# A Fourier mixing layer and a routed expert layer on one core: GpSimd's time in the planner's due times, the tile ramp made once, a larger reserve of expert work

## The chip, the cores and the metric

The kernel runs on one core of a Trainium2 chip. The metric is device time in microseconds (us). The time before is the median of three runs. Everything is float32. Engine names are those of the profile: PE (TensorE matmuls), PEld (its weight loads), DVE (VectorE), ACT (ScalarE), POOL (GpSimd), SP (SyncE, which here issues the ordinary DMAs).

## The reference, cut to what matters

```python
# x (8, 2496, 256), filt_r and filt_i (1249, 256)
X = np.fft.rfft(x, axis=1)
Y = X * (filt_r + 1j * filt_i)[None]
x = np.fft.irfft(Y, n=2496, axis=1).astype(np.float32).reshape(19968, 256)
# w_gate (256, 8), w1 (8, 256, 1024), w2 (8, 1024, 256)
logits = x @ w_gate
expert_idx = np.argmax(logits, axis=1)
probs = softmax(logits)                      # with 1e-9 added to the sum
gate_w = probs[np.arange(N), expert_idx]
for e in range(8):                           # on the tokens of expert e
    y[tokens] = np.maximum(x[tokens] @ w1[e], 0.0) @ w2[e]
return gate_w[:, None] * y                   # (19968, 256)
```

## The kernel before, in words

**Fourier part.** A sequence of 2496 is cut as 39 by 64, and the transform is done with four kinds of matmul steps for each of the 8 batches. `stage_a` (line 324) does the 39-point transforms, `stage_b` (line 337) the 64-point ones with the twiddle factors, followed on DVE by the product with the filter; `stage_c` (line 361, and 359 for the first pair) goes back over 64 points and `stage_d` (line 382) over 39. Between A and B the data makes a round trip through DRAM (`zd`), between C and D another (`ud`), and D's result is stored to `yd`. `turn_y` (line 395) transposes it and `logits` (line 408) multiplies it by the gate weights. The loads land in tiles called `fin` (8 buffers); what A, C and D leave for their stores (`zo`, `uo`, `yo`) shares 6 buffers, so the copy out of PSUM for a seventh such tile waits for the first one's stores.

**Routing.** When a batch is done, `route` turns its logits into a row of a table in DRAM for each token. It has a chain of small DVE operations, two matmuls `rk` (lines 444 and 445) in the midst of it, and at its end 22 indirect DMAs on GpSimd (line 485), each of which scatters 8 bytes for each of up to 117 tokens (30 DMAs in the last batch). Then `tile_map` works out, in one-row DVE operations, which expert and which table row each tile of 512, 256 or 128 tokens has. There are 65 tiles: 1, 6, 2, 5, 5, 5, 5 and 36 for the eight batches, which are called batch 0 to batch 7 here.

**Experts.** For a tile, SP reads its list of tokens from the table (`listed`, line 574, into `idt`). Its DMA waits for all the scatters that stand before it in the program. GpSimd gathers the tokens' rows from `yd` (`gather`, line 590, one indirect DMA for 128 rows, into `xg`, 2 buffers), PE transposes them (`turn_x`, line 617), multiplies by the expert's `w1` (`hidden`, line 624) and by `w2` (`result`, line 639), and GpSimd scatters the gated rows to the output (line 644). The weights, 1 MB each for a tile, are loaded by SP (lines 609 and 605).

**What sets the order.** The program is a planner that writes out PE, DVE, ACT and SP by hand, in the order in which it runs; on GpSimd a scheduler keeps nearly the same order. The loop at the end takes one step after the other, either of the Fourier part or of the experts, and advances a clock `now` by the step's price (for instance 0.43 us for a `hidden` of 128 columns, 3.42 for a `result`). An expert step may be taken when the thing it needs is due: `prefetch` notes in `when`, at each issue, `now` plus a constant of `GAP` (5 us for a list, 7 for a gather, 9 for weights). `share` says how much expert work goes between Fourier steps, from what is known and not done, less `RESERVE`. After each step, `side` is called twice and advances `route` or `tile_map` to its next `yield`.

Of the kernel before, what the change touches and what calls it, by code (L numbers as in the profile page):

```python
# [10 lines left out]
F32 = mybir.dt.float32  # L11
I32 = mybir.dt.int32
U32 = mybir.dt.uint32
AF = mybir.ActivationFunctionType
ALU = mybir.AluOpType
# [7 lines left out]
E = 8  # L23
# [110 lines left out]
def kernel(  # L134
# [15 lines left out]
    nc = tc.nc  # L150
# [9 lines left out]
    for b in range(B):  # L160
        GROUPS.append([])
        for rows, most in WANT[b]:
            n = min(most, max(0, ((b + 1) * S - (N - left) - E * (rows - 1)) // rows))
# [14 lines left out]
    perm = ctx.enter_context(tc.tile_pool(name="perm", bufs=1))  # L178
# [3 lines left out]
    eoff = perm.tile([P, E], F32, name="eoff")  # L182
    done = perm.tile([1, E], F32, name="done")
    one = perm.tile([1, E], F32, name="one")
    moe = ctx.enter_context(tc.tile_pool(name="moe", bufs=2))
    ps = ctx.enter_context(tc.tile_pool(name="ps", bufs=7, space=PSUM))

    fft = ctx.enter_context(ExitStack())
    cst = fft.enter_context(tc.tile_pool(name="cst", bufs=1))
# [15 lines left out]
    ids0 = cst.tile([TP, NG], F32, name="ids0")  # L205
    vld = cst.tile([TP, NG], F32, name="vld")
    e_i = cst.tile([P, E], I32, name="e_i")

    def bank():
        return ps.tile([P, 512], F32, tag="bank", name="bank")  # L210


    now = [0.0]
    free = {"v": 0.0, "s": 0.0}

    def either(n, on_vector, on_scalar):

        v = max(free["v"], now[0]) + 0.1 + n / 960
        s = max(free["s"], now[0]) + 0.2 + n / 1200
        if v <= s:  # L220
            free["v"] = v
            on_vector()
        else:
            free["s"] = s
            on_scalar()

    def evac(o, i, n):
        either(n, lambda: nc.vector.tensor_copy(o, i), lambda: nc.scalar.copy(out=o, in_=i))  # L228

    HP = P // 2  # L230
    CH = [(i0, min(4, NG - i0)) for i0 in range(0, NG, 4)]
# [22 lines left out]
    def make_constants():  # L254
        make_identity(nc, ident)
        nc.gpsimd.memset(ones, 1.0)
        nc.gpsimd.affine_select(
            out=tri, in_=ones[:, :TP], compare_op=ALU.is_gt, fill=0.0, base=0, pattern=[[1, TP]], channel_multiplier=-1
        )
        nc.gpsimd.memset(seg, 1.0)  # L260
        nc.gpsimd.memset(seg[:, :, 0:1], 0.0)
        nc.gpsimd.memset(cnt, 0.0)
        nc.gpsimd.memset(fill[:, 0:1], N)
        nc.gpsimd.memset(fill[:, 1:2], 0)
        nc.gpsimd.iota(prow, pattern=[[0, 1]], base=0, channel_multiplier=1)
        nc.gpsimd.iota(e_i, pattern=[[1, E]], base=0, channel_multiplier=0)
        nc.vector.tensor_scalar(em8, in0=e_i, scalar1=-float(E), scalar2=None, op0=ALU.add)
        nc.vector.tensor_scalar(eoff, in0=e_i, scalar1=float(TE), scalar2=None, op0=ALU.mult)
        nc.vector.memset(done, 0.0)
        nc.vector.memset(one, 1.0)  # L270
# [17 lines left out]
    def mark(key):  # L288
        moves[1].append(lambda: stored.add(key))
# [118 lines left out]
                    mm(lgs[b][:TP, 0, t * E:(t + 1) * E], lhsT=yt[:, 2 * i + dh, :], rhs=wg[:, dh, :],  # L408
                       start=(dh == 0), stop=(dh == DH - 1))

    scatters = {}


    def route(b):
# [3 lines left out]
        she = (TP, E, NG)  # L418
# [55 lines left out]
        rows = [(row[:N1 if t == NG - 1 else TP, t:t + 1], pay[:N1 if t == NG - 1 else TP, t, :]) for t in range(NG)]  # L474
        if b == B - 1:
# [5 lines left out]
            nc.vector.tensor_copy(pad, padf)  # L481
            rows += [(pad[:, e:e + 1], fill) for e in range(E)]
        scatters[b] = []
        for t, (at, what) in enumerate(rows):
            sc = nc.gpsimd.indirect_dma_start(  # L485
                out=table,
                out_offset=bass.IndirectOffsetOnAxis(ap=at, axis=0),
                in_=what,
                in_offset=None,
            )  # L490

            tc.declare_no_dep(sc.ins, group="scatter", reason="rows of their own")
            tc.declare_no_dep(sc.ins, group="listed", reason="rows of their own")
            tc.add_to_no_dep_group("scatter", sc.ins)
            scatters[b].append(sc.ins.name)
            if t % 2:
                yield


    def tile_map(b, rows, n, last):  # L500
# [3 lines left out]
        end = moe.tile([1, E], F32, name="end", bufs=1)  # L504
# [14 lines left out]
        nc.vector.tensor_tensor(add, add, base, op=ALU.subtract)  # L519
        nc.vector.tensor_tensor(add[:, :E - 1], add[:, :E - 1], base[:, 1:], op=ALU.add)  # L520
        yield
        tau_i = moe.tile([1, n], I32, tag=f"tau_i{n}", name="tau_i", bufs=1)
        tau = moe.tile([1, n], F32, tag=f"tau{n}", name="tau", bufs=1)
        nc.gpsimd.iota(tau_i, pattern=[[1, n]], base=0, channel_multiplier=0)
        nc.vector.tensor_copy(tau, tau_i)
        past = moe.tile([1, n, E - 1], F32, tag=f"past{n}", name="past", bufs=1)
        she = (1, n, E - 1)
        nc.vector.tensor_tensor(
            past, tau[:, :, None].to_broadcast(she), end[:, None, :E - 1].to_broadcast(she), op=ALU.is_ge
        )  # L530
        yield
        ef = moe.tile([1, n], F32, tag=f"ef{n}", name="ef", bufs=1)
# [5 lines left out]
        rf = moe.tile([1, n], F32, tag=f"rf{n}", name="rf", bufs=1)  # L538
        rrow = moe.tile([1, n], I32, tag=f"rrow{n}", name="rrow", bufs=2)
        nc.vector.tensor_reduce(rf, past, axis=AX.X, op=ALU.add)  # L540
        nc.vector.tensor_scalar(tau, in0=tau, scalar1=float(rows), scalar2=base[:, 0:1], op0=ALU.mult, op1=ALU.add)
        nc.vector.tensor_tensor(rf, rf, tau, op=ALU.add)
        if last:

# [86 lines left out]
    def result(i, j):  # L631
        n, e, r, b = work[i]
        ids = idt[i]
        if i >= SHORT:
            ev = nc.tensor.value_load(e, min_val=0, max_val=E - 1)
        p = bank()
        for k in range(FT):
            w2 = late["w2s"][:, bass.ds(ev, 1), k, :] if i >= SHORT else w2t[i][:, k, :]
            mm(p[:, :D], lhsT=hs[i][k][:, j * P:(j + 1) * P], rhs=w2, start=(k == 0), stop=(k == FT - 1))  # L639
        ys = moe.tile([P, D], F32, tag="ys", name="ys", bufs=4)  # L640
        gate = ids.bitcast(F32)[:, j, 1:2]
        either(D, lambda: nc.vector.tensor_scalar(ys, in0=p[:, :D], scalar1=gate, scalar2=None, op0=ALU.mult),  # L642
               lambda: nc.scalar.activation(ys, p[:, :D], AF.Copy, scale=gate))
        nc.gpsimd.indirect_dma_start(  # L644
            out=out,
            out_offset=bass.IndirectOffsetOnAxis(ap=ids.bitcast(U32)[:, j, 0:1], axis=0),
            in_=ys,
            in_offset=None,
            bounds_check=N - 1,
            oob_is_err=False,  # L650
        )
# [74 lines left out]
    got = {"list": 0, "x": 0, "w1": 0, "w2": 0}  # L726
    used = {"x": 0, "w1": 0, "w2": 0}
    when = {}
    GAP = {"list": 5.0, "x": 7.0, "w1": 9.0, "w2": 9.0}

    def prefetch():

        def may(what, depth):
            i = got[what]
            deep = depth if i < SHORT else 4
            return i < len(work) and i - used.get(what, used["w1"]) < deep
        def mark(what):
            when[what, got[what]] = now[0] + GAP[what]
            got[what] += 1
        if may("list", 3):  # L740
            listed(got["list"])
            mark("list")
        i = got["x"]
        if i < got["list"] and i - used["x"] < 2 and when["list", i] <= now[0]:
            gather(i)
            mark("x")
        for what in ("w1", "w2"):
            if got[what] < got["list"] and may(what, 2):
                weights(got[what], what == "w2")
                mark(what)  # L750
# [23 lines left out]
        return min(4.0, max(0.3, (known - RESERVE) / max(left_t[0], 1.0)))  # L774


    RESERVE = 40.0
    with tc.manual_schedule(
        engines={mybir.EngineType.PE, mybir.EngineType.DVE, mybir.EngineType.Activation, mybir.EngineType.SP}
    ):  # L780
# [62 lines left out]
```

## Time and profile before

| | |
|---|---|
| median of 3 runs | 1778.86 us (1777.88 to 1785.63) |
| profiled execution: its own time | 1779.41 us |
| profiled execution: span of the instructions | 1777.7 us |
| mean granted TensorE clock | 0.954 |
| PE busy | 1618.0 us, 91% of the span, 7126 records |
| DVE, ACT, POOL busy | 554.2, 318.0, 504.3 us |
| DMA | 296.16 MB, mean 167 GB/s |

In the records of PE a float32 matmul of the program stands as two, a transposition as one. Busy time of PE is not yet work done, since a matmul takes about twice as long while the granted clock is 0.5. So the profile is read in two steps: where PE stands idle and for whom, and at which clock it worked afterwards.

### The profile page before, as it was taken

Reading aid. Unit: us, or ns where it says so; the run is one execution under the profiler, and the core shown is the slowest. Engines: PE = TensorE matmul, PEld = TensorE weight load, DVE = VectorE, ACT = ScalarE, POOL = GpSimd, SP = SyncE. Lnnn points to the kernel's source line nnn. Section 1 sums busy time; section 2 is a strip of 40 time slices with the busy share of each in tenths; the row PEclk is TensorE's granted clock in tenths of the full one; section 3 lists DMA queues with packets and bytes.
Section 4 is the critical chain, followed back from the end, with each engine's and each line's share of the span. In section 5 each row is a group of like instructions: output and inputs, shape, how many; then the busy total and the mean of one; then the engine's idle time right before and its main releaser. Section 6 shows DMA issues by size and latency. Waiting matters only on the chain.

```text
span 1777.7 us, 21069 instructions
## 1 busy us (share of the span) xinstructions
PE 1618.0 (91%) x7126; PEld 1183.5 (67%) x7126; DVE 554.2 (31%) x1328; ACT 318.0 (18%) x575; POOL 504.3 (28%) x536
## 2 busy tenths in 40 slices
PE   3897695999997899979999799999999999999997
PEld 1464463877665566656676567676767668889997
DVE  0755362255351112512125122313101002334443
ACT  1332121122221122212222121212121210000000
POOL 0003123215225220342115312445523222222221
PEclk7898897999998899989999899999999999999999
DMA  8888778568758452754425523542434335554551
GB/s 298 259 258 206 220 185 236 199 188 205 240 120 195 149 184 75 183 175 135 123 91 129 177 97 110 147 139 81 131 140 174 145 132 186 193 197 168 176 178 42
DMA packets 120965, 296.16 MB, mean 167 GB/s; under 512 B 32338, under 2 KB 73028, under 8 KB 105893
## 3 DMA queue, kind: packets, MB, share of 16 engines
q1 hardware_dynamic: 99322, 252.77, 47.0%
q0 software_dynamic: 21536, 42.03, 7.4%
q8 instruction: 58, 0.95, 0.2%
q14 instruction: 49, 0.40, 0.1%
HBM read 212.74 MB, written 82.88 MB: 166 GB/s over the span
## 4 chain that ended last, share of the span: by engine, by line
PE 76%; DMA 11%; issue 4%; POOL 4%; DVE 3%; SPq 1%; ACT 0%; POOLq 0%; DVEq 0%; ACTq 0%
PE bank L639 30%; PE bank L624 29%; PE lg L408 3%; POOL table L485 3%; PE bank L337 3%; DMA fin<-ud 3%; PE bank L382 2%; PE bank L361 2%; PE bank L324 2%; DMA xg<-yd,idt 2%; PE bank L617 2%; DMA zd<-zo 2%; PE bank L395 2%; DMA table<-pay,row 1%; DMA ud<-uo 1%
## 5 line engine op out<-in xcount | busy, mean ns | idle before, releaser
L624 PE MATMUL bank<-xT,w1t 128*128 128x512 f32 (+2 forms) x2080 | 595.4, 438 | 0.1
L639 PE MATMUL bank<-w2t,hT 128*128 128x256 f32 x2240 | 502.2, 382 | 0.0
L624 PEld LDWEIGHTS bank<-xT,w1t 128*128 128x128 f32 x2080 | 340.1, 192 | 203.9 <-issue 183.8
L639 PEld LDWEIGHTS bank<-w2t,hT 128*128 128x128 f32 x2240 | 424.8, 191 | 61.9 <-issue 5.3
L644 POOL DMA_INDIRECT out_dram<-ys,idt x163 | 162.6, 998 | 683.4 <-DVE ys L642 352.0
L485 POOL DMA_INDIRECT table<-pay,row x176 | 173.5, 986 | 289.0 <-DVE row L471 184.7
L590 POOL DMA_INDIRECT xg<-yd,idt x163 | 157.6, 967 | 288.8 <-PE bank L617 201.7
L628 ACT ACTIVATE hT<-bank 128x512 f32<-128x512 f32 (+1 forms) x235 | 138.0, 587 | 490.2 <-PE bank L624 490.2
L642 DVE TENSOR_SCALAR ys<-bank,idt 128x256 f32<-128x256 f32 x150 | 72.5, 483 | 482.4 <-PE bank L639 454.6
L617 PE MATMUL bank<-ident,xg 128*128 128x128 f32 x326 | 53.8, 292 | 77.3 <-DMA xg<-yd,idt 77.1
L627 DVE TENSOR_SCALAR hT<-bank 128x128 f32<-128x128 f32 (+1 forms) x285 | 96.5, 339 | 80.7 <-PE bank L624 77.6
L337 PE MATMUL bank<-fin,tbs 128*128 128x256 f32 (+1 forms) x320 | 90.4, 405 | 26.0 <-issue 25.1
L228 DVE COPY xT<-bank 128x512 f32<-128x512 f32 (+2 forms) x64 | 30.9, 483 | 266.1 <-PE bank L617 266.1
L617 PEld LDWEIGHTS bank<-ident,xg 128*128 128x128 f32 x326 | 41.3, 148 | 96.5 <-issue 82.7
L382 PE MATMUL bank<-fin,tds 117*117 117x256 f32 (+1 forms) x352 | 89.2, 393 | 15.4 <-DMA fin<-ud 15.4
L337 PEld LDWEIGHTS bank<-fin,tbs 128*128 128x128 f32 (+1 forms) x320 | 61.1, 199 | 58.1 <-issue 47.7
L324 PE MATMUL bank<-fin,tas 117*117 117x512 f32 x176 | 91.6, 647 | 6.2 <-DMA fin<-in_x_dram 6.1
L382 PEld LDWEIGHTS bank<-fin,tds 117*117 117x117 f32 (+1 forms) x352 | 64.4, 187 | 46.5 <-issue 27.5
L228 ACT COPY xT<-bank 128x512 f32<-128x512 f32 (+2 forms) x66 | 28.1, 428 | 370.3 <-PE bank L617 266.3
L344 DVE TENSOR_TENSOR ys<-bank,ht 128x512 f32<-128x512 f32 x80 | 55.1, 688 | 123.1 <-PE bank L337 123.0
L408 PEld LDWEIGHTS lg<-wg,yt 128*117 128x117 f32 x704 | 79.5, 183 | 9.7 <-issue 5.6
L361 PE MATMUL bank<-ys,tcs 128*128 128x512 f32 x144 | 75.2, 604 | 10.3 <-DVE ys L347 6.9
(97 smaller groups left out, 893.0 us busy)
## 6 DMA issues: line engine op xcount, KB each, us to landing
w1t<-in_moe_w_dram SPq DMA_DIRECT2D x65, 1024.0 KB
w2t<-in_moe_w_dram SPq DMA_DIRECT2D x42, 1024.0 KB
fin<-in_x_dram SPq DMA_DIRECT2D x40, 512.0 KB
zd<-zo SPq DMA_DIRECT2D x120, 156.0 KB
fin<-ud SPq DMA_DIRECT2D x120, 156.0 KB
yd<-yo SPq DMA_DIRECT2D x120, 156.0 KB
fin<-zd SPq DMA_DIRECT2D x72, 256.0 KB
ud<-uo SPq DMA_DIRECT2D x72, 256.0 KB
```

What stands on the lines that cost most here:

```text
L324: mm(p[:TP, :], lhsT=tas, rhs=xt[:TP, j:j + 2, :], start=True, stop=True)
L337: mm(p[:, i * D:(i + 1) * D], lhsT=tbs[:k, f + i, :], rhs=zi[:k, j + i, :], start=True, stop=True)
L361: mm(p, lhsT=tcs[:, 1, :], rhs=ys, start=True, stop=True)
L382: mm(p[:TP, i * D:(i + 1) * D], lhsT=tds[:k, i0 + j + i, :], rhs=ui[:k, j + i, :], start=True, stop=True)
L408: mm(lgs[b][:TP, 0, t * E:(t + 1) * E], lhsT=yt[:, 2 * i + dh, :], rhs=wg[:, dh, :], start=(dh == 0), stop=(dh == DH - 1))
L485: sc = nc.gpsimd.indirect_dma_start(out=table, out_offset=bass.IndirectOffsetOnAxis(ap=at, axis=0), in_=what, in_offset=None,)
L590: nc.gpsimd.indirect_dma_start(out=xgs[i][:, j], out_offset=None, in_=yd[0:rows, :], in_offset=bass.IndirectOffsetOnAxis(ap=idt[i].bitcast ...
L617: nc.tensor.transpose(pt[:, j, :], xg[:, j, dh * P:(dh + 1) * P], ident)
L624: mm(p[:, :m], lhsT=w1t[i][:, dh, k * P:(k + 1) * P], rhs=xts[i][:, dh, :m], start=(dh == 0), stop=(dh == DH - 1))
L628: lambda: nc.scalar.activation(hT[:, :m], p[:, :m], AF.Relu))
L639: mm(p[:, :D], lhsT=hs[i][k][:, j * P:(j + 1) * P], rhs=w2, start=(k == 0), stop=(k == FT - 1))
L644: nc.gpsimd.indirect_dma_start(out=out, out_offset=bass.IndirectOffsetOnAxis(ap=ids.bitcast(U32)[:, j, 0:1], axis=0), in_=ys, in_offset=No ...
```

## The change

It has four parts. The constants of `GAP` for lists and gathers go, and the planner keeps a clock for GpSimd (`free["p"]`, advanced by `pool`, 1.3 us for each indirect DMA): a list is due 5 us after the scatters of its batch are, a gather 3.5 us after GpSimd's clock has passed it. `route` gives control back after 8 scatters instead of 2, so that the 22 scatters stand in the program in one or two places instead of six, and `tile_map` and the batch's first lists come earlier. The ramp 0, 1, 2, ... that `tile_map` needs is made once at the start (`tau0`), where each call had made its own on GpSimd and cast it on DVE. `RESERVE` goes from 40 to 60 us.

```diff
+    tau0 = perm.tile([1, 64], F32, name="tau0")
...
-    free = {"v": 0.0, "s": 0.0}
+    free = {"v": 0.0, "s": 0.0, "p": 0.0}
...
+    def pool(start, n):
+
+        free["p"] = max(free["p"], start) + 1.3 * n
+        return free["p"]
...
+        nc.gpsimd.iota(tau_i, pattern=[[1, 64]], base=0, channel_multiplier=0)
+        nc.vector.tensor_copy(tau0, tau_i)
...
         scatters[b] = []
+        rows_at[b] = pool(now[0] + 5.0, len(rows)) + 3.0
...
-            if t % 2:
+            if t % 8 == 7:
                 yield
...
-        tau_i = moe.tile([1, n], I32, tag=f"tau_i{n}", name="tau_i", bufs=1)
         tau = moe.tile([1, n], F32, tag=f"tau{n}", name="tau", bufs=1)
-        nc.gpsimd.iota(tau_i, pattern=[[1, n]], base=0, channel_multiplier=0)
-        nc.vector.tensor_copy(tau, tau_i)
...
         gate = ids.bitcast(F32)[:, j, 1:2]
+        pool(now[0], 1)
...
-    GAP = {"list": 5.0, "x": 7.0, "w1": 9.0, "w2": 9.0}
...
-        def mark(what):
-            when[what, got[what]] = now[0] + GAP[what]
+        def mark(what, at=None):
+            when[what, got[what]] = at or now[0] + 9.0
             got[what] += 1
         if may("list", 3):
-            listed(got["list"])
-            mark("list")
+            i = got["list"]
+            listed(i)
+            mark("list", max(now[0], rows_at[work[i][3]]) + 5.0)
...
             gather(i)
-            mark("x")
+            mark("x", pool(now[0], work[i][0]) + 3.5)
...
-    RESERVE = 40.0
+    RESERVE = 60.0
```

What this does to the order is shown at three places. The names are those of the profile; the line numbers of the changed kernel are 7 to 9 higher, so that its `turn_x` is L624, its `hidden` L631 and its `result` L646. A row stands for one kind of instruction, with its count behind the x.

The first place is PE in the routing of batch 4, up to the transposition of that batch's first tile (the last row). In the kernel before, these are the last twelve of the 21 rows that follow `rk`:

```order
L361 MATMUL bank<-ys,tcs 128x512
L382 MATMUL bank<-fin,tds 117x256 x4
L395 MATMUL bank<-ident,yo 128x117 x8
L324 MATMUL bank<-fin,tas 117x512 x2
L624 MATMUL bank<-xT,w1t 128x512 x6
L337 MATMUL bank<-fin,tbs 128x256 x2
L624 MATMUL bank<-xT,w1t 128x512 x4
L361 MATMUL bank<-ys,tcs 128x512
L624 MATMUL bank<-xT,w1t 128x512 x4
L382 MATMUL bank<-fin,tds 117x256 x4
L624 MATMUL bank<-xT,w1t 128x512 x2
L617 MATMUL bank<-ident,xg 128x128 x8
```

In the changed kernel, the last twelve of the 29 rows that follow `rk`, up to the same tile:

```order
L404 MATMUL bank<-ident,yo 128x117 x8
L646 MATMUL bank<-w2t,hT 128x256 x8
L333 MATMUL bank<-fin,tas 117x512 x2
L646 MATMUL bank<-w2t,hT 128x256 x8
L631 MATMUL bank<-xT,w1t 128x512 x4
L346 MATMUL bank<-fin,tbs 128x256 x2
L631 MATMUL bank<-xT,w1t 128x512 x2
L370 MATMUL bank<-ys,tcs 128x512
L631 MATMUL bank<-xT,w1t 128x512 x4
L391 MATMUL bank<-fin,tds 117x256 x4
L631 MATMUL bank<-xT,w1t 128x512 x6
L624 MATMUL bank<-ident,xg 128x128 x8
```

Before the batch's first transposition there now stand a whole `hidden` and a whole `result` of the tile ahead of it and a part of the next tile's `hidden`.

The second place is SP in the routing of batch 0, around the batch's first list (`idt`). Before:

```order
L316 DMA fin<-ud 39x4x256 x3
L286 DMA yd<-yo 39x1024 x3
L309 DMA fin<-zd 64x1024
L310 DMA fin<-zd 64x1024
L286 DMA zd<-zo 39x4x256 x3
L303 DMA fin<-in_x_dram 128x512
L316 DMA fin<-ud 39x4x256 x3
L286 DMA yd<-yo 39x1024 x3
L316 DMA fin<-ud 39x2x256
L316 DMA fin<-ud 39x256 x2
L572 TENSOR_LOAD rrow
L572 ISA x2
```

And in the changed kernel, from the same load of `ud` on:

```order
L325 DMA fin<-ud 39x4x256 x3
L295 DMA yd<-yo 39x1024 x3
L318 DMA fin<-zd 64x1024
L319 DMA fin<-zd 64x1024
L579 TENSOR_LOAD rrow
L579 ISA x2
L581 ISA
L581 DMA idt<-table 128x4
L609 TENSOR_LOAD erow
L609 ISA x2
L616 ISA
L616 DMA w1t<-in_moe_w_dram 128x2048
```

The list has moved ahead of a store of `zd`, a load of `x`, two loads of `ud` and a store of `yd`, which now follow it and the two weight loads.

The third place is SP in the routing of batch 1. Before, from a load of `x` on:

```order
L303 DMA fin<-in_x_dram 128x1024
L286 DMA zd<-zo 39x4x256 x3
L286 DMA ud<-uo 64x1024
L286 DMA ud<-uo 64x768
L316 DMA fin<-ud 39x4x256 x3
L286 DMA yd<-yo 39x1024 x3
L309 DMA fin<-zd 64x1024
L310 DMA fin<-zd 64x1024
L286 DMA zd<-zo 39x4x256 x3
L303 DMA fin<-in_x_dram 128x512
L316 DMA fin<-ud 39x4x256 x3
L286 DMA yd<-yo 39x1024 x3
```

And in the changed kernel, from the same load on:

```order
L312 DMA fin<-in_x_dram 128x1024
L579 TENSOR_LOAD rrow
L579 ISA x2
L581 ISA
L581 DMA idt<-table 128x8
L609 TENSOR_LOAD erow
L609 ISA x2
L616 ISA
L616 DMA w1t<-in_moe_w_dram 128x2048
L609 TENSOR_LOAD erow
L609 ISA x2
L612 ISA
```

Before, the list of batch 1 follows these twelve rows; now it stands right behind the load of `x`, and all the stores and loads of the other rows follow it.

## Rows read from the trace of the kernel before

**Rows 1.** Waits of PE: who waited for whom, us, times, longest.
```profile
PE bank L617 <- DMA xg<-yd,idt: 77.1, 17, 16.1
```
**Rows 2.** Timeline of PE, batches 1, 3, 4: start, length, what, records, idle before.
```profile
244.79 0.53 PE L444 MATMUL rk<-oe,tri 117*117 117x176 f32 x2 [2.12 <-DVE oe L435]
...
515.39 0.59 PE L444 MATMUL rk<-oe,tri 117*117 117x176 f32 x2 [2.12 <-DVE oe L435]
...
585.04 1.33 PE L617 MATMUL bank<-ident,xg 128*128 128x128 f32 x5 [0.64 <-DMA xg<-yd,idt]
...
732.17 0.53 PE L444 MATMUL rk<-oe,tri 117*117 117x176 f32 x2 [2.38 <-DVE oe L435]
...
739.73 3.62 PE L639 MATMUL bank<-w2t,hT 128*128 128x256 f32 x16
743.18 1.88 PE L324 MATMUL bank<-fin,tas 117*117 117x512 f32 x4
744.90 1.03 PE L337 MATMUL bank<-fin,tbs 128*128 128x256 f32 x4
745.77 1.02 PE L361 MATMUL bank<-ys,tcs 128*128 128x512 f32 x2
746.63 1.89 PE L382 MATMUL bank<-fin,tds 117*117 117x256 f32 x8
748.36 0.96 PE L395 MATMUL bank<-ident,yo 117*128 117x117 f32 x8
749.15 1.88 PE L324 MATMUL bank<-fin,tas 117*117 117x512 f32 x4
750.88 5.31 PE L624 MATMUL bank<-xT,w1t 128*128 128x512 f32 x12
756.03 1.03 PE L337 MATMUL bank<-fin,tbs 128*128 128x256 f32 x4
...
780.20 0.45 PE L617 MATMUL bank<-ident,xg 128*128 128x128 f32 x1 [11.98 <-DMA xg<-yd,idt]
```
**Rows 3.** Timeline of POOL, batch 4: first and last scatter, ramp, first gather.
```profile
739.18 0.98 POOL L485 DMA_INDIRECT table<-pay,row  x1 [10.58 <-DVE row L471]
...
767.51 0.89 POOL L485 DMA_INDIRECT table<-pay,row  x1 [0.30 <-issue]
768.42 0.13 POOL L524 IOTA tau_i<- 1x5 int32 x1
...
772.79 0.99 POOL L590 DMA_INDIRECT xg<-yd,idt  x1 [4.24 <-DMA idt<-table]
```
**Rows 4.** Five stretches: length, busy (records) PE PEld DVE ACT POOL, clock, DMA.
```profile
189.30:208.50 19.20, 3.87 (x12) 2.95 (x12) 1.54 (x3) 2.03 (x4) 1.96 (x2) 0.56 0.81 280
282.00:304.10 22.10, 4.44 (x11) 2.31 (x11) 1.38 (x2) 2.25 (x4) 6.20 (x8) 0.61 0.79 262
565.00:590.80 25.80, 7.21 (x15) 3.49 (x15) 0.69 (x1) 1.18 (x2) 12.87 (x14) 0.54 0.85 279
768.20:785.40 17.20, 4.15 (x13) 3.01 (x13) 0.69 (x1) 1.18 (x2) 4.18 (x6) 0.60 0.77 245
978.90:997.00 18.10, 6.47 (x19) 4.76 (x19) 0.69 (x1) 1.18 (x2) 3.84 (x4) 0.62 0.74 259
```
**Rows 5.** SP's line of the lists: semaphore waits, ns min/median/max; scatters' time to landing.
```profile
L574 SPq EVENT_SEMAPHORE  x122: 17/28/26921, 192.8 to 1728.4; - x122
...
DMA to landing us min/median/max: 2.5/7.7/12.5
```
**Rows 6.** Timelines of SP and POOL, batches 0 and 1: list's new neighbour, last scatter.
```profile
180.88 0.79 SPq L310 DMA_DIRECT2D fin<-zd  x1
...
182.21 0.90 POOL L485 DMA_INDIRECT table<-pay,row  x1 [0.30 <-issue]
...
257.14 0.36 SPq L303 DMA_DIRECT2D fin<-in_x_dram  x1
...
282.18 0.89 POOL L485 DMA_INDIRECT table<-pay,row  x1 [0.30 <-DMA zd<-zo]
```
**Rows 7.** A stretch of Fourier work alone, columns as in rows 4.
```profile
100.00:145.00 45.00, 41.47 (x220) 29.81 (x218) 27.01 (x46) 14.49 (x27) 0.00 (x0) 0.96 0.85 255
```

More of the change, by code (lines that the diff above doesn't have):

```diff
@@ L207 @@
     e_i = cst.tile([P, E], I32, name="e_i")
+    tau_i = cst.tile([1, 64], I32, name="tau_i")
     def bank():
@@ L409, in logits @@
                        start=(dh == 0), stop=(dh == DH - 1))
-    scatters = {}
+    scatters, rows_at = {}, {}
     def route(b):
@@ L528, in tile_map @@
         nc.vector.tensor_tensor(
-            past, tau[:, :, None].to_broadcast(she), end[:, None, :E - 1].to_broadcast(she), op=ALU.is_ge
+            past, tau0[:, :n, None].to_broadcast(she), end[:, None, :E - 1].to_broadcast(she), op=ALU.is_ge
         )
@@ L540, in tile_map @@
         nc.vector.tensor_reduce(rf, past, axis=AX.X, op=ALU.add)
-        nc.vector.tensor_scalar(tau, in0=tau, scalar1=float(rows), scalar2=base[:, 0:1], op0=ALU.mult, op1=ALU.add)
+        nc.vector.tensor_scalar(tau, in0=tau0[:, :n], scalar1=float(rows), scalar2=base[:, 0:1], op0=ALU.mult, op1=ALU.add)
         nc.vector.tensor_tensor(rf, rf, tau, op=ALU.add)
```

## The prediction

> **What bounds the kernel now.** PE is busy 91% of the span, so I looked first for whom it waits. One line of that list is large: the first transposition of a tile, which waits for its gathered rows, 77.1 us in 17 waits [rows 1]. The timeline of PE shows where. In batch 4, `rk` starts at 732.17, and at 780.20 the first transposition comes after 11.98 us of idling [rows 2]. The timeline of POOL says why: the first scatter starts 7 us after `rk`, the last at 767.51, and the gather can only start at 772.79, when the list has been read [rows 3]. From the first scatter to the last, 767.51 - 739.18 = 28.3 us go for 22 indirect DMAs (one output scatter among them), 1.29 us each, and that is most of the way. The same happens in batches 0, 1, 3 and 5, and after each stop the clock is at 0.5 for some us more. Rows 4 has the five stretches, each from PE's stop to the clock's return.
>
> What such a stretch loses is its length less the work done in it. The busy part lies at half clock, so the work is half of it: 19.2 - 1.9 = 17.3, 22.1 - 2.2 = 19.9, 25.8 - 3.6 = 22.2, 17.2 - 2.1 = 15.1 and 18.1 - 3.2 = 14.9 us [rows 4]. Together that is 89.4 us: 37.2 in batches 0 and 1, 52.2 in batches 3, 4 and 5.
>
> **How much work stands between.** The prices of PE's steps are differences of starts [rows 2]: `result` 3.45 for 16 records, A 1.72 for 4, B 0.87 for 4, C 0.86 for 2, D 1.73 for 8, `turn_y` 0.79 for 8, `hidden` 5.15 for 12. In matmuls of the program (two records each, a transposition one) that is 0.43 for B, D and `result`, 0.86 for A, C and a `hidden` of 512 columns, 0.10 for a `turn_y`; a transposition of 128 columns I take at 0.14. In batch 4 before, there stand between `rk` and the first transposition of the batch's first tile 16 `hidden` (13.8), 8 `result` (3.4), 6 A (5.2), 8 B (3.5), C for 3.4, 12 D (5.2), `turn_y` 0.8 and `rk` 0.6, in all 36 us. From 732.17 on that ends at 768.2, and that is where PE stops (780.20 - 11.98). So the prices hold, and what decides is this cover against the 48 us that the gathers took.
>
> In the changed order the same place has 32 `hidden` (27.5), 32 `result` (13.8), a tile's transpositions (1.1) and the same Fourier steps: 61 us. Counted in the same way, the cover before and after is 28 and 52 us in batch 0, 30 and 54 in 1, 61 and 93 in 2, 48 and 63 in 3, 36 and 61 in 4, 36 and 61 in 5, 59 and 68 in 6, 124 and 126 in 7.
>
> **The change part by part.** *Due times for lists and gathers.* In batch 4 the gathers' data came 48 us after `rk` began and the last piece some 2.5 us later; 61 covers that with 10 to spare. Batch 5 is alike. In batch 3 the last piece came at 585.04, 69.7 us after `rk` [rows 2], because output scatters stood between on POOL. 63 us do not cover that. But the list stands earlier now and the output scatters that still stand between belong to work that PE has done before, so I take zero there and 7 us as the bad end. So the 52.2 us of the three late batches go. In batches 0 and 1 the gathers' waits of 37.2 us go too, since 52 and 54 us of work at that place take longer than 52 us on the clock: PE took from 244.79 to 282.0, 37.2 us, for 29.7 us of such work [rows 2, 4].
>
> *Scatters in one place, lists earlier.* This is what the change adds. SP's instruction for the list waits until the scatters that stand before it have landed, and everything behind it on SP waits too. Such a wait lasted up to 26.9 us before [rows 5]. In batch 0 SP reaches the list's new place at 181.7 (the end of the `zd` load); the last scatter starts at 182.21 and lands 2.5 us (least) to 7.7 us (median) later, so SP stands for 3 to 8 us [rows 5, 6]. In batch 1 the new neighbour is the `x` load at 257.14, the last scatter starts at 282.18: SP stands for 27 to 32 us, until 40 to 45 us after `rk` [rows 5, 6]. Behind it wait stores of `zd` and `ud`, loads of `ud`, `zd` and `x`, and the weights.
>
> What PE can do meanwhile follows from the order. The first step that needs something behind the list comes 24 us of PE work after `rk` in batch 0 (a copy into the six shared buffers, whose `zd` store waits), 29 in batch 1 (the same, with a `ud` store), 54 in batch 2, 77 to 80 in batches 3 to 6, and 55 in batch 7, where only weights wait. A small DMA that was issued behind two weight loads took 780.20 - 772.79 = 7.4 us [rows 2, 3]. So the missing thing is there 47 to 52 us after `rk`: in time for batches 2 to 6, too late for 0 and 1. In batch 7 thirty scatters make it 8 x 1.29 = 10 us later, 57 to 62 against 55, for a weight load that is two tiles ahead in the order; I take zero and 6 as the bad end. Batch 0: PE reaches its place about 4 us before 189.3 [rows 4], at 185, and gets on at 192 to 197; 7 to 12 us, I take 8. Batch 1: it reaches 29 us of work about 36 us after `rk` and gets on at 47 to 52; 11 to 16, I take 13. After each, some 2 us at half clock, as in rows 4. In all 25 us given back. The values are near the short ends because SP and the transfers run late in these batches anyway.
>
> The Trainium skill ("DMA: Bandwidth & Descriptors", Anatomy of one DMA) says that DMA engines do not wait on semaphores and that any such wait happens on the issuing sequencer before dispatch. By that rule the wait stops the whole queue, and the 26.9 us of rows 5 agree; if the wait went along with its own DMA, the 25 us would fall away and the sum would be 1693.
>
> *A larger reserve.* PE's work is the same in amount and no path gets longer by it; it moves expert work from batches 0 to 2 to later. In batch 0, 52 instead of 28 us of nearly pure Fourier work follow `rk`. Such work runs at 41.47 / 45 = 0.92 busy and a clock of 0.96, so at 0.885 of full rate, beside a DMA share of 0.85 [rows 7]. 24 us more of it lose 24 / 0.885 - 24 = 3 us; the ends are 0 (if it fills holes that experts would fill) and 9 (three batches).
>
> *The ramp.* Eleven short instructions each on POOL and DVE become one. One took 0.13 us on POOL [rows 3], right behind the last scatter, where POOL then waits for the list; zero, and 10 x 0.13 = 1 us if that cover went. `tile_map`'s DVE operations come a few steps earlier in DVE's queue, the same in number, on an engine that is busy 31% of the span; zero.
>
> **Sum**, against the profiled execution's own 1779.4 us (0.6 above the median, so I make no difference): 1779.4 - 89.4 + 25 + 3 = 1718.
>
> **The rivals.** *A: the early gain is eaten up.* The transfers are the limit in batches 0 and 1 (share 0.79 to 0.85 in rows 4 and 7), so that what PE no longer waits for gathers it waits for `ud`, `zd` and stores. Then only the late 52.2 us go, less up to 7 in batch 3 and some 10 for a longer stop: 1727 to 1750, about 1737. For it speaks that SP's queue stands 30 us in a stage with little expert work; against it that PE was busy 0.92 of the time in a stretch of Fourier work alone, so that the transfers nearly keep up [rows 7].
>
> *B: nothing is given back.* SP's stops lie beside queued transfers, as those of 26.9 us did in the kernel before. 1779.4 - 89.4 = 1690, with 0 to 9 for the thinner mix up to 1699.
>
> *C: slower.* SP's stop reaches PE in every batch. The point from which it decides: the list is released later than PE can work, so beyond 77 us after `rk` instead of 40 to 45. Then six batches lose 26.9 + 2 us and batch 0 some 8: 1779.4 - 89.4 + 6 x 28.9 + 8 + 3 = 1874. Nothing in the order speaks for it, unless scatters land far later than 7.7 us.
>
> *D: the due times do not do what they say.* The gathers stay as late relative to PE as before, because POOL stands behind output scatters longer than 1.3 us each, as in batch 3. Half of the late 52.2 stays: 1744.
>
> *E: no difference*, because other work moves into the stops and is missed later: 1775 to 1785. Against it, PE's idle time has no other large owner [rows 1].
>
> **How the numbers follow.** The forecast (1700 to 1735) 0.53; A 0.21; B 0.12; C 0.05; D 0.05; E 0.04. The range takes in the forecast, A to its end and nearly all of B: 1692 to 1750. A measurement of this kernel tells about 0.5%, 9 us, from no change: faster 0.90, within 0.04, slower 0.06.
>
> **What would show it.** Right: in the profile after, PE's waits for `xg` under 15 us in all, none of more than 7 in batches 3 to 5, and the clock at full from some 400 us on; SP's waits at the list near 27 us in most batches; two new idle places of PE of 8 and 13 us in batches 0 and 1, for loads, or for DVE or ACT with a store before them. Wrong: stops of PE for `fin` or weights in batches 3 to 7 (C); `xg` still over 30 us (D); `rk` of batch 2 no earlier on the clock for the same amount of work done (A).

## The result, and the profile after

The changed kernel takes 1723.6 us (median of 4 runs, 1719.3 to 1731.9) against 1779.2 for the kernel before: ratio 0.969, 95% interval 0.964 to 0.973. The forecast was 1718. The profiled execution of the changed kernel is the longest of its four, 1731.9 us of its own time with a span of 1730.2, so it is to be read against 1779.4 of before: 47.5 us less.

PE's list of waits, the one that rows 1 are from (who waited for whom; us in all, times, longest), no longer has a line for `xg`. Of the longest that are left behind the start, the three lines that end in `ACT zo` or `ACT yo` are new; before, such a wait came to 0.2 us in all:

```profile
PE bank L404 <- ACT zo L230: 17.8, 2, 15.2
PE rk L453 <- DVE oe L444: 11.5, 5, 3.0
PE bank L391 <- DMA fin<-ud: 11.4, 4, 4.5
...
PE bank L370 <- ACT zo L230: 8.5, 1, 8.5
PE bank L391 <- ACT yo L230: 5.4, 2, 4.5
```

Line 230 is the copy out of PSUM, here into the six shared `st` buffers: PE stands because ACT stands, and ACT stands because a buffer's store has not gone out, as ACT's timeline shows for the second stop:

```profile
291.64 0.59 ACT L230 COPY zo<-bank 117x512 f32<-117x512 f32 x1 [21.19 <-DMA zd<-zo]
```

The timeline of PE (start, length, what, records, idle time before) has the three places, one in batch 0 and two in batch 1, and then batch 4, where [rows 2] had an idle time of 11.98 us ahead of the first transposition:

```profile
205.50 2.08 PE L370 MATMUL bank<-ys,tcs 128*128 128x512 f32 x2 [8.45 <-ACT zo L230]
...
292.28 1.04 PE L404 MATMUL bank<-ident,yo 117*128 117x117 f32 x4 [15.24 <-ACT zo L230]
...
309.93 2.29 PE L391 MATMUL bank<-fin,tds 117*117 117x256 f32 x5 [4.54 <-ACT yo L230]
...
688.31 0.53 PE L453 MATMUL rk<-oe,tri 117*117 117x176 f32 x2 [2.12 <-DVE oe L444]
...
750.88 1.04 PE L624 MATMUL bank<-ident,xg 128*128 128x128 f32 x8
```

In batch 4 the first transposition now comes 62.6 us after `rk` and has waited for nothing. On POOL the same place reads like this; [rows 3] answers to it, with the gather 40.6 us after `rk`, here it is 49.3:

```profile
725.24 0.90 POOL L495 DMA_INDIRECT table<-pay,row  x1 [0.30 <-issue]
...
737.57 1.00 POOL L597 DMA_INDIRECT xg<-yd,idt  x1 [0.30 <-PE bank L631]
```

Batch 1 shows what stands behind the new stops. The first fence is SP's timeline, the second the busy time by stretch (columns as in [rows 4]):

```profile
252.92 1.09 SPq L312 DMA_DIRECT2D fin<-in_x_dram  x1
277.66 0.37 SPq L581 DMA_DIRECT2D idt<-table  x1
278.83 0.35 SPq L616 DMA_DIRECT2D w1t<-in_moe_w_dram  x1
```

```profile
261.80:279.40 17.60, 15.24 (x80) 12.17 (x78) 2.61 (x5) 1.61 (x3) 11.23 (x12) 1.00 0.04 8
279.40:296.50 17.10, 4.04 (x10) 2.66 (x11) 4.76 (x8) 2.60 (x5) 5.41 (x6) 0.50 0.92 301
```

Between the `x` load and the list SP issues nothing for 23.7 us. For 17.6 us of that the DMA engines are all but empty (share 0.04, 8 GB/s) while PE works off what it has; then everything comes at once (0.92, 301 GB/s) and PE stands, at half clock. The Trainium skill ("DMA: Bandwidth & Descriptors", Anatomy of one DMA) has the wait for a semaphore on the issuing sequencer; the 0.04 agrees.

To see where time is lost I use one more measure below: **lateness**, the moment at which PE has done so many us of work, less that amount. The work is counted from PE's records at their full-clock prices (a matmul of 512 columns 0.86, of 256 0.43, and so on; 1573 us in all, in every kernel). It is read at batch 0's `rk` (88 us of work), at 350 us, and at PE's end.

| kernel | at 88 | at 350 | at the end | 88 to 350 | 350 to the end |
|---|---|---|---|---|---|
| before | 57 | 130 | 194 | 73 | 64 |
| after | 61 | 135 | 146 | 74 | 11 |

So in these two executions the whole gain lies behind 350 us of work, 53 us, and the early part gained nothing: the gathers' waits of batches 0 and 1 have gone, and as much has come in their place. Up to batch 0's `rk` PE's order is the same in both kernels, so the 4 us there (57 to 61) are not the change's. Below, such kernels with one order up to there differ by up to 5 us, and a difference of that size says nothing. The three parts, 53 - 1 - 4, explain the profiled 1731.9; the median is 8 us less, and no trace from this chip tells in which part. Over the late part, 330 to 1600 us, PE's busy time rose by 45 us and its clock by 0.02 (first before, then after):

```profile
330.00:1600.00 1270.00, 1213.15 (x5046) 871.55 (x5045) 342.54 (x800) 237.01 (x419) 401.41 (x412) 0.97 0.50 153
```

```profile
330.00:1600.00 1270.00, 1258.40 (x5378) 916.43 (x5377) 352.92 (x847) 240.17 (x430) 416.00 (x423) 0.99 0.50 159
```

### The profile page after: what moved, and what is told of

It reads as the page before. It is cut to its first block, busy times and chain, and to the rows that moved or that the text cites. A ratio compares the mean times of both kernels' runs of the same rounds, so it can differ in the third digit from the quotient of the medians.

```text
span 1730.2 us, 21068 instructions
## 1 busy us (share of the span) xinstructions
PE 1621.2 (94%) x7126; PEld 1186.8 (69%) x7126; DVE 549.2 (32%) x1312; ACT 319.6 (18%) x581; POOL 503.8 (29%) x526
## 4 chain that ended last, share of the span: by engine, by line
PE 80%; DMA 2%; DVE 1%; issue 0%; SPq 0%; ACT 0%; POOLq 0%; ACTq 0%
PE bank L631 32%; PE bank L646 32%; PE bank L391 3%; PE lg L417 3%; PE bank L346 2%; PE bank L624 2%; PE bank L370 2%; PE bank L404 1%; PE bank L333 1%; DMA ud<-uo 1%; DMA yd<-yo 0%; DMA zd<-zo 0%; PE bank L368 0%; DMA fin<-ud 0%; PE rk L453 0%
## 5 line engine op out<-in xcount | busy, mean ns | idle before, releaser
L631 PE MATMUL bank<-xT,w1t 128*128 128x512 f32 (+2 forms) x2080 | 588.6, 435 | 1.8 <-DVE yo L230 1.2
L646 PE MATMUL bank<-w2t,hT 128*128 128x256 f32 x2240 | 498.6, 380 | 0.0
L631 PEld LDWEIGHTS bank<-xT,w1t 128*128 128x128 f32 x2080 | 339.2, 191 | 210.0 <-issue 188.4
L646 PEld LDWEIGHTS bank<-w2t,hT 128*128 128x128 f32 x2240 | 420.6, 190 | 59.7 <-issue 4.9
L346 PE MATMUL bank<-fin,tbs 128*128 128x256 f32 (+1 forms) x320 | 95.4, 423 | 26.5 <-issue 25.2
L391 PE MATMUL bank<-fin,tds 117*117 117x256 f32 (+1 forms) x352 | 93.8, 410 | 16.8 <-DMA fin<-ud 11.4
L370 PE MATMUL bank<-ys,tcs 128*128 128x512 f32 x144 | 79.5, 636 | 13.8 <-ACT zo L230 8.5
L646 PE MATMUL bank<-w2s,hT 128*128 x368 | 83.2, 379 | 0.0
L417 PE MATMUL lg<-wg,yt 128*117 128x8 f32 x704 | 77.9, 245 | 0.0
```

Source lines behind the costliest of these rows:

```text
L346: mm(p[:, i * D:(i + 1) * D], lhsT=tbs[:k, f + i, :], rhs=zi[:k, j + i, :], start=True, stop=True)
L370: mm(p, lhsT=tcs[:, 1, :], rhs=ys, start=True, stop=True)
L391: mm(p[:TP, i * D:(i + 1) * D], lhsT=tds[:k, i0 + j + i, :], rhs=ui[:k, j + i, :], start=True, stop=True)
L631: mm(p[:, :m], lhsT=w1t[i][:, dh, k * P:(k + 1) * P], rhs=xts[i][:, dh, :m], start=(dh == 0), stop=(dh == DH - 1))
```

## The experiments

They ran on three other chips, on which the kernel before takes 1800 to 1804 us. Ratios are to that. All lateness is from one profiled execution each:

| kernel | us (ratio, 95%) | at 88 | at 350 | at the end | 88 to 350 | 350 to the end |
|---|---|---|---|---|---|---|
| before | 1800.8 | 59 | 142 | 215 | 83 | 73 |
| after | 1731.2 (0.958 to 0.967) | 57 | 133 | 146 | 76 | 13 |
| due times alone | 1760.8 (0.975 to 0.980) | 58 | 131 | 175 | 73 | 44 |
| reserve alone | 1742.9 (0.963 to 0.968) | 59 | 140 | 157 | 81 | 17 |
| both, scatters spread | 1730.4 (0.956 to 0.965) | 58 | 128 | 144 | 70 | 16 |
| list held back | 1738.8 (0.962 to 0.967) | 57 | 121 | 155 | 64 | 34 |
| lists on GpSimd | 1729.2 (0.957 to 0.962) | 56 | 121 | 143 | 65 | 22 |
| fewer weights early | 1725.6 (0.956 to 0.964) | 58 | 124 | 133 | 66 | 9 |
| 22 more scatters, 8 bytes | 1734.9 (0.958 to 0.967) | 82 | 150 | 159 | 68 | 9 |
| the same, 512 bytes | 1731.6 (0.958 to 0.964) | 64 | 142 | 156 | 78 | 14 |
| GpSimd's lists, 0 to 6 | 1723.0 (0.955 to 0.958) | 59 | 121 | 136 | 62 | 15 |
| and a wide table | 1697.5 (0.939 to 0.944) | 58 | 101 | 112 | 43 | 11 |

### What made the late gain: due times or reserve

Due times alone: the changed kernel with two edits undone.

```
-            if t % 8 == 7:
+            if t % 2:
...
-    RESERVE = 60.0
+    RESERVE = 40.0
```

> The kernel before with the due times alone (ramp made once, too): scatters spread as before, reserve 40. PE's cover between rk and the first transposition is 52, 54, 62, 55, 57, 57, 59, 124 us of work. Theory 1: the gathers took about 50 us, so the late 52 us go; the early part is as in the changed kernel; 1715 to 1730. Rival, the reserve made the late gain: PE runs out of expert work instead and the late stretches keep half of their loss or more, 1745 to 1770.

The reserve alone: the kernel before with `RESERVE = 60.0`.

> The kernel before with the larger reserve alone. Cover 28, 30, 94, 64, 65, 65, 92, 146 us: the early batches as before, the late ones covered by the stock of expert work even without due times. Theory 1 (only the cover counts, whoever makes it): the late 52 us go, the early 37 stay, 1724 to 1735. Rival, the due times made the late gain: 1765 to 1780.

Both, with the scatters spread as before (the changed kernel with the first of the two edits above):

> The changed kernel with the scatters spread again (two to a step, as before), so that the first list of a batch stands later in SP's order (15 and 13 us of PE's work behind rk in batches 0 and 1 instead of 9 and 7); due times and reserve as changed, cover 52, 54, 93, 64, 65, 63, 86, 133 us. Theory 1, the SP stop: 5 to 15 us faster than the changed kernel. Theory 2, transfers: the same within 5 us.

Late loss 73 before, 44 with due times alone, 17 with the reserve alone, 16 and 13 with both. So the reserve by itself brings nearly all of it, and due times less than half. By time, the reserve alone, one constant, has a ratio of 0.966 (0.963 to 0.968), which the intervals do not tell from the whole change, 0.962 (0.958 to 0.967) on these chips and 0.969 on the first (1724 to 1735 had meant 0.969 to 0.975); in the traces it ends 11 us behind the changed kernel. The rival was right for due times: 0.977, where 1715 to 1730 meant 0.964 to 0.972; they don't reach the time that the cover promised. Their timelines of POOL and PE in batch 4 (`rk` at 725.04) say why:

```profile
777.79 0.98 POOL L652 DMA_INDIRECT out_dram<-ys,idt  x1 [6.54 <-issue]
781.76 0.98 POOL L652 DMA_INDIRECT out_dram<-ys,idt  x1 [2.99 <-DMA idt<-table]
783.05 1.00 POOL L597 DMA_INDIRECT xg<-yd,idt  x1 [0.31 <-issue]
```

```profile
790.77 0.99 PE L624 MATMUL bank<-ident,xg 128*128 128x128 f32 x2 [6.79 <-DMA xg<-yd,idt]
```

The cover rose from 36 to 57 us of work, and the gather moved too: it starts 58 us after `rk`, not 40.6, behind output scatters of rows that PE finished in the meantime, and the rows are there at 65.7. The order that covers the gather also delays it. With the reserve alone (`rk` at 698.69) the gather of batch 4 moves just as far, to 56 us after `rk` and behind four output scatters:

```profile
753.41 0.98 POOL L644 DMA_INDIRECT out_dram<-ys,idt  x1 [3.43 <-DMA idt<-table]
754.70 0.99 POOL L590 DMA_INDIRECT xg<-yd,idt  x1 [0.31 <-PE bank L624]
```

```profile
765.43 0.49 PE L617 MATMUL bank<-ident,xg 128*128 128x128 f32 x3
```

But here the cover is 64 to 65 in batches 3 to 5, and PE comes to the transposition 66.7 us after `rk`, when the rows have just landed: a cover of 65 reaches over the delayed gather and one of 57 does not. Of the reserve's `xg` waits, 39.2 us, 15.4 and 21.3 lie in batches 0 and 1.

Spreading the scatters changes 1 us of 1731, within the error of both; of the 76 us of early loss it takes 6. With intervals of 8 us to either side this run does not tell theory 1 from theory 2.

### What takes the place of the early waits

Theory 1 was SP's stop at the list, theory 2 the transfers as such. Two kernels take the stop from SP. In the first the list enters SP's order when the scatters are due:

```
-        if may("list", 3):
-            i = got["list"]
+        i = got["list"]
+        if may("list", 3) and now[0] >= rows_at[work[i][3]]:
```

> The changed kernel, but the list of a batch's first tile is put into SP's order only when the order's clock has reached the time at which the scatters are due, so that SP does not stand in front of them (in batches 0 and 1 the list moves from 9 and 7 us of PE work behind rk to 40). Theory 1, the SP stop: the three stops of PE after rk in batches 0 and 1 (8.5, 15.2 and 4.5 us, ended by ACT's copies into the shared buffers) go, with some 10 us of half clock, and the time falls by 25 to 35 us, to 1690 to 1700. Theory 2, the transfers are the limit while Fourier work runs: PE waits as long for fin or for stores elsewhere, the first 350 us of PE's work still end some 130 us late, and the time stays at 1715 to 1730.

In the second GpSimd reads the list:

```
-        r0 = nc.sync.value_load(r, min_val=0, max_val=TR - n * P)
+        r0 = nc.gpsimd.value_load(r, min_val=0, max_val=TR - n * P)
...
-        ld = nc.sync.dma_start(
+        ld = nc.gpsimd.dma_start(
```

> The changed kernel, but the lists are read by a DMA that GpSimd issues, so that the wait for the scatters stands in GpSimd's queue and SP never waits for it; the order of PE is the same. Theory 1, the SP stop: as with the held list, 25 to 35 us less, 1690 to 1700, less what GpSimd's own stop costs (its scatters of finished rows stand behind; four buffers cover them): up to 1705. Theory 2, transfers are the limit: 1715 to 1730, and PE's stops in batches 0 and 1 move to other loads and stores.

The changed kernel beside them, for its own time on these chips:

> The changed kernel, unaltered, beside the variants: 1718 to 1750 and 0.965 to 0.972 of the kernel before; its first 350 us of PE's work end some 130 to 135 us late.

Both take 12 us off the lateness at 350, a third to a half of the 25 to 35 that theory 1 had. Neither is faster than the changed kernel by more than the intervals. With the held list the stops behind ACT in batches 0 and 1 are all but gone, as theory 1 had it (1.5 us of them are left, of 10.2 + 16.3 + 4.1 in the changed kernel). But the hold has a price of its own, already in the early part: in batch 0 the last scatter is issued at 183.88, SP comes to the list at 222.72, and by then POOL has six of the next batch's scatters ahead of the gather, so that PE stands 20 us. So its 12 us are what is left after that price, and do not measure SP's stop. Behind 350 it loses 21 us more than the changed kernel: in batches 3 to 5 the gather starts 58 to 61 us after `rk`, and PE waits 4 to 5 us in each. These are SP's, POOL's and PE's timelines of that kernel in batch 0:

```profile
222.72 0.39 SPq L581 DMA_DIRECT2D idt<-table  x1
```

```profile
229.20 0.98 POOL L495 DMA_INDIRECT table<-pay,row  x1 [44.42 <-DVE av L515]
...
236.95 0.98 POOL L597 DMA_INDIRECT xg<-yd,idt  x1 [0.30 <-issue]
```

```profile
244.95 0.45 PE L624 MATMUL bank<-ident,xg 128*128 128x128 f32 x1 [20.19 <-DMA xg<-yd,idt]
```

With the lists on GpSimd there is no such delay, and yet PE stands in the same places, 3.9, 9.7 and 5.3 us instead of 10.2, 16.3 and 4.1. What fills them, if SP never stops? Theory 2 was tried by taking transfers away: tiles 1 to 6 use the weights of tile 0.

```
+        if 0 < i < 7:
+            (w2t if second else w1t)[i] = (w2t if second else w1t)[0]
+            return
```

> The changed kernel with 12.6 MB less to read while Fourier work runs: the expert tiles 1 to 6 (batches 0 and 1) use the weights loaded for tile 0, so their outputs are those of another expert; every instruction of PE and every wait for scatters stays. Theory 1, the SP stop: the stops of PE in batches 0 and 1 stay, time within 5 us of the changed kernel. Theory 2, the transfers are the limit in the first 320 us: 12.6 MB at the 0.2 to 0.28 MB per us of that part are 45 to 60 us of transfer, and PE gets back 20 to 40 us of them.

9 us less at 350 and 6 us less in time, for 12.6 MB, and the three stops are still there (9.3, 8.7 and 3.1 us): less than the 20 to 40 us of theory 2, so the amount of bytes isn't the whole answer either.

### Scatters of 8 bytes slow the other transfers

In the changed kernel the DMA engines are busy and move little while batch 0's scatters run: 0.94 busy at 163 GB/s from 150 to 180 us, against 0.94 at 273 from 95 to 120. That became theory 3. Twenty-two more scatters (the text on record says twenty), to a table that nothing reads, were put where PE does Fourier work alone:

```
+    def extra():
+        nc.vector.tensor_copy(xpay[:TP], outs["o", 0, 0][:, 0, 0:2])
+        for t in range(NG):
+            sc = nc.gpsimd.indirect_dma_start(
+                out=xtab,
+                out_offset=bass.IndirectOffsetOnAxis(ap=xrow.bitcast(U32)[:TP, t:t + 1], axis=0),
+                in_=xpay[:TP],
+                in_offset=None,
+            )
...
```

> The changed kernel with twenty more scatters of the same size to a table that nothing reads, started when the first tile of batch 0's output stands (some 95 us into the span, 50 us before the first real ones), while PE does Fourier work alone. Nothing waits for them. Theory 3, scatters slow the transfers (in the traces packets of 1 KB take 103 to 123 ns while scatters run against 54 before): the stretch with them moves 165 to 185 GB/s instead of 225 to 285, and PE loses 8 to 15 us. Otherwise (only waiting for scatters costs): no loss, within 3 us.

And the same with rows of 512 bytes (`in_=ht[:TP, 0, :P]`, and a table of that width; it starts 2.8 us sooner):

> As the run with twenty more scatters, at the same place, but each row that they write has 512 bytes instead of 8 (a constant, read from the filter's tile): the same count of rows and of GpSimd instructions. If it is the number of rows or GpSimd's issuing that slows the transfers, PE loses the same 25 us up to batch 0's rk (rk at 167 to 172 again). If it is that rows of 8 bytes are written, rk comes at 145 to 152.

The stretch 95 to 120 us of the changed kernel, of the one with 8-byte scatters and of the one with 512-byte scatters (columns as in [rows 4]; POOL is the fifth, the last two are DMA share and GB/s):

```profile
95.00:120.00 25.00, 22.44 (x114) 16.10 (x115) 9.98 (x15) 7.55 (x14) 0.00 (x0) 1.00 0.94 273
```

```profile
95.00:120.00 25.00, 18.70 (x75) 12.18 (x74) 5.51 (x9) 6.27 (x12) 16.90 (x17) 0.77 1.04 179
```

```profile
95.00:120.00 25.00, 22.16 (x109) 15.39 (x108) 9.99 (x15) 7.64 (x14) 19.21 (x20) 1.00 0.96 285
```

The DMA engines are about as busy in all three. With rows of 8 bytes they move 179 GB/s, with rows of 512 bytes 285, but part of this is the scatters' own. The same 25 us by queue (packets, MB, share of the 16 engines' time; `q1` has what SP issues, `q0` the scatters), without scatters, with 8 and with 512 bytes:

```profile
q1 hardware_dynamic: 4496, 6.82, 93.4%
```

```profile
q1 hardware_dynamic: 2935, 4.45, 102.0%
q0 software_dynamic: 466, 0.02, 1.7%
```

```profile
q1 hardware_dynamic: 3976, 6.04, 80.8%
q0 software_dynamic: 842, 1.08, 15.0%
```

So SP's transfers go from 273 GB/s to 178 beside 8-byte rows, and to 242 beside 512-byte rows, which take 43 themselves. With 8 bytes PE does 75 matmul records instead of 114, and `rk` comes at 170.2 instead of 144.7; with 512 bytes at 152.0, so that these cost some 7 us as well. The scatters' own time from issue to landing is 10.6 us (median) against 5.5. GpSimd's pace is 1.29 us in both (with 8 bytes it stood 3.4 us more, for landings), so it is not the issuing. I had expected a loss of 8 to 15 us at `rk`; it was 25. At PE's end both kernels with more scatters are 10 to 13 us later than the one without, and their times don't differ from it: this pair shows the slower transfers, not a price for the whole kernel. That comes from the next two.

### A version that is faster than both

GpSimd reads the lists of batches 0 to 6, SP those of batch 7, where GpSimd's stop had cost some us:

```
+        by = nc.gpsimd if b < B - 1 else nc.sync
```

> The changed kernel with GpSimd reading the lists of batches 0 to 6, and SP those of batch 7, where GpSimd's stop had cost 9 us between 1050 and 1300 us of PE's work. The early part as with all lists on GpSimd (12 us less lost than in the changed kernel), the late part as in the changed kernel: 10 to 15 us faster than the changed kernel, 1715 to 1722 on this chip, 0.955 to 0.958 of the kernel before.

And with that, a table whose rows are 512 bytes wide. A scatter reads 512 bytes per row, of which the first 8 count; a list reads these 8. To make room, `pos` and `run` use the buffers of `ex` and `oh`.

```
-    table = dram.tile([TR, 2], I32, tag="table", name="table")
+    table = dram.tile([TR, P], I32, tag="table", name="table")
...
+    payw = cst.tile([TP, 2 * NG - 2 + P], I32, name="payw")
...
-        pay = sb.tile([TP, NG, 2], I32, tag="pay", name="pay", bufs=1)
+        pay = payw[:, :2 * NG].rearrange("p (t c) -> p t c", c=2)
...
-        rows = [(row[:N1 if t == NG - 1 else TP, t:t + 1], pay[:N1 if t == NG - 1 else TP, t, :]) for t in range(NG)]
+        rows = [(row[:N1 if t == NG - 1 else TP, t:t + 1], payw[:N1 if t == NG - 1 else TP, 2 * t:2 * t + P]) for t in range(NG)]
...
-            out=idt[i][:, :n], in_=table[bass.ds(r0, n * P), :].rearrange("(p i) c -> p i c", i=n)
+            out=idt[i][:, :n], in_=table[bass.ds(r0, n * P), 0:2].rearrange("(p i) c -> p i c", i=n)
```

> As the run with GpSimd reading the lists of batches 0 to 6, and the table's rows are 512 bytes wide instead of 8: a scatter writes whole rows (the first 8 bytes count, the rest is whatever stands behind them in SBUF), and a list reads 8 bytes of each row. PE's order is the same. If the 8-byte rows are what slows the transfers in batches 0 and 1, the stretches with scatters move 250 MB per ms or more at 1 KB packets of some 55 ns, the first 350 us of PE's work end 10 to 25 us sooner (96 to 111 us late instead of 121), and the time is 1700 to 1715, ratio 0.943 to 0.951. Against it: a list becomes 512 reads of 8 bytes instead of 128 of 32; if those cost as the writes did, the time stays at 1720 or rises.

1723.0 and 1697.5, on two chips on which the kernel before takes 1804 and 1803. The first is 8 us below the changed kernel, where 10 to 15 were expected. The second is 0.941 of the kernel before (0.939 to 0.944), a little under what was expected. The lateness at 350 falls from 121 to 101, and the stretches with scatters say it again: 150 to 180 and 240 to 270 us, first with GpSimd's lists and rows of 8 bytes, then with wide rows.

```profile
150.00:180.00 30.00, 20.67 (x65) 12.86 (x63) 13.06 (x42) 5.62 (x10) 17.29 (x18) 0.84 0.91 180
...
240.00:270.00 30.00, 25.13 (x119) 19.36 (x117) 12.93 (x42) 3.79 (x8) 18.52 (x19) 0.99 1.06 181
```

```profile
150.00:180.00 30.00, 23.59 (x95) 15.33 (x94) 18.78 (x52) 8.28 (x16) 20.20 (x20) 0.94 0.92 260
...
240.00:270.00 30.00, 28.57 (x145) 21.72 (x143) 12.10 (x20) 7.14 (x13) 16.07 (x18) 1.00 0.95 298
```

180 and 181 GB/s became 260 and 298. Without what GpSimd's own DMAs move, SP's transfers went from 180 to 224 and from 179 to 269. Of PE's waits for ACT's copies, 27.3 us with GpSimd's lists (12.4 + 10.0 + 4.9), 10.7 are left:

```profile
PE bank L372 <- ACT zo L231: 5.9, 1, 5.9
PE bank L393 <- ACT yo L231: 4.8, 2, 4.5
```

If the lists' smaller pieces (8 bytes instead of 32) cost anything, it is less than that. What a width between 8 and 512 bytes would do, and the wide table with the lists left on SP, were not run.

Last, the kernel before on one of these chips, since it is 22 us slower there and the changed kernel only 8:

> The kernel before, unaltered, for its trace on the chip on which the variants ran (there its time is 1800, not 1779). If the 22 us lie where PE waits for gathered rows, the waits for xg are above 77 us here and the first 350 us of PE's work end as late as in the first trace (130 us); if the transfers of the early part are slower on this chip, the 22 us are already lost there (150 us).

Both: 12 us more at 350 and 9 more behind it, with 84.6 us of waits for `xg` instead of 77.1. Why gathers and transfers are slower there stays open; it is the reason to compare with the kernel before on the same chip only.

## Why the prediction was right, and where it was not

**The late 52.2 us: right in size.** Behind 350 us of work the changed kernel lost 53 us less than before (64 to 11), 60 on the second chip. The signs named for it came: no wait for `xg`, the clock at full behind 400 us but for 3.4 us near the `rk` of batches 3 to 6 and the last 9 us. The price was right because the cover of the finished order, 61 to 63 us, was counted for all edits together, and because 36 and 48 us were read from the trace.

**Whose it is: wrong.** The step "due times for lists and gathers" takes all of it. By the runs alone, due times bring 29 of the 73 us on the other chips and the reserve 56. The step set a grown cover against gathers that stay 48 us (50 with the last piece) behind `rk`; under due times the rows came at 65.7, and with the reserve alone no sooner, against a cover that is 8 us larger. The reserve was priced as a loss of 3 us by a thinner mix; the early loss with the reserve alone, 81 against 83, shows no such loss. Had the reserve not been in the change, the 52.2 would have been some 23 us too much.

**The early 37.2 less 25 less 3: mis-sized.** The sum had a gain of 9 there; the first chip's two traces have none (73 to 74), those of the second 7 (83 to 76). The stops were at the predicted places, of the predicted kind, and near the predicted length: 8.45 against 8 in batch 0, 15.24 against 13 in batch 1, and a third of 4.54 that I had not seen. The term that was too small is the 25. These are the three stretches in the way of [rows 4], from PE's stop to the clock's return:

```profile
197.05:221.40 24.35, 15.07 (x42) 10.48 (x43) 6.38 (x10) 4.32 (x8) 0.76 (x1) 0.58 0.88 278
277.04:296.50 19.46, 4.04 (x10) 2.66 (x11) 4.76 (x8) 2.60 (x5) 5.41 (x6) 0.56 0.82 269
305.39:313.60 8.21, 3.67 (x12) 2.83 (x11) 3.91 (x6) 1.53 (x3) 0.00 (x0) 0.79 0.95 333
```

Length less half of the busy time is 16.8 us in batch 0, where the sum had 8 + 2, and 17.4 in batch 1, where it had 13 + 2; the third adds 6.4. Together that is 40.6 us instead of 25, more than the 37.2 that the gathers' stops had cost. On the second chip the three lose 40.4. The step "after each, some 2 us at half clock" held in batch 1 (half of 4.04) and failed in batch 0: PE worked 15.07 us at 0.50 behind that stop, with one wait of 0.83 us, which costs 7.5. I had taken the 2 from the gathers' stops. Why the clock came back 16 us after the end of one stop and 4 after that of the next, no run shows.

**SP's stop: a true mechanism, its share not settled.** With the lists on GpSimd the early loss falls by 11 to 14 us, not by 25; wide rows then take 19 more. The held list took nearly all of the stops behind ACT away, but put one of its own in their place. What the prediction did not have is that scatters slow the transfers while they run. [Rows 4] and [rows 7], from which it judged the transfers, show 245 to 280 GB/s; the stretch with batch 0's scatters, which it did not read, has 180 at a share of 0.93:

```profile
150.00:180.00 30.00, 20.12 (x75) 13.44 (x73) 11.69 (x41) 4.81 (x9) 19.25 (x20) 0.83 0.93 180
```

The kernel before has these scatters too, and with a wide table it was not run. So the 19 us are what narrow rows cost in the order with GpSimd's lists; that they are why the 25 was too small is not shown.

**Rival A** ("the early gain is eaten up") said this of the early part, with a loss of 10 for a longer stop in the late part that did not come: 1779.4 less the 52.2, without that 10, would have been 1727. Its sign was that the same work is done no earlier by batch 2's `rk`, and it isn't: 250 us of work stand at 374 us before and at 385 after. So the profiled execution is the forecast's late part with rival A's early part. The median of 1723.6 lies 6 us from the sum and inside the range, closer than the parts deserve, and that is luck: the late gain came from an edit that was priced as a loss, and the early gain of 9 is missing in the trace.

**B** (nothing given back) fell by the stops themselves, **C** by batches 3 to 7: SP's list waits there were 15 to 30 us in four of them and 48 in the last, and PE waited for none. **D** fell for the whole change, by the missing `xg` line, and was half true of due times by themselves. **E** fell by the time. The ramp was taken at zero and was not run by itself.

## What to carry to other kernels

When a wait on a critical path is covered by an order that also moves the waiting thing, price both ends: how much work now stands before the use, and when the thing now starts. Read GB/s beside the DMA share: engines that are 0.9 busy at two thirds of their usual rate have a cause of their own, and it may be somebody's small writes. And a stop can cost more than its length: one of 8.5 us cost 16.8 here, because the clock stayed at half for 16 us behind it. Last, run each edit by itself: here one constant brought most of what four parts together did.

## What the runs showed of the hardware

Indirect scatters of 22 times 117 rows of 8 bytes, 0.02 MB in all, brought the core's other transfers from 273 to 178 GB/s while they ran, with the DMA engines 1.04 busy; beside rows of 512 bytes, 64 times the bytes, these moved 242 GB/s and the scatters 43. The Trainium skill ("DMA: Bandwidth & Descriptors", Specifications) asks for at least 512 bytes for line rate and has a read-modify-write below that; the two widths measured here agree, and the runs add that the neighbours' rate suffers too. No run here shows the threshold.

A queue that stands at one wait can leave all 16 DMA engines empty: 0.04 busy for 17.6 us.
